# Expert 0's weights in smaller loads, and its first down product taken by halves of the contraction

## The chip, the cores and the metric

The kernel runs on one core of a Trainium2 chip. The metric is the device time of one execution in microseconds. Each comparison uses executions of both kernels, in rounds on the same chip. A ratio below is the mean time of one kernel's fast runs over the mean of the other's in the same rounds, so it is not quite the ratio of the medians that are quoted beside it.

## The reference, cut to what matters

```python
# q, k, v: 8 batches x 8 heads x 576 positions x 64
ret = (q @ k.T / 8) * decay ** (i - j)    # lower triangle only
x = (ret @ v) as 4608 tokens x 512
p = domain_probs / domain_probs.sum(-1)   # 4608 x 4
for e in range(4):                        # w1[e]: 512 x 1024, w2[e]: 1024 x 512
    h = relu(x @ w1[e])                   # "up"
    out += p[:, e] * (h @ w2[e])          # "down"
```

The kernel does batch 0's attention first (the head of the program, some 18 us), then the experts on the first tile of 512 tokens, with later batches' attention mixed in. Expert 0's weights are therefore the first that TensorE asks for, and they come from memory while the raw q, k and v of batch 0 are still arriving.

## The kernel before

```python
def load_w1(e, f=slice(0, F)):            # f32 in memory, bf16 as written
    return nc.gpsimd.dma_start(out=w1_sb[e][:, :, f], in_=moe_w1[e][:, f]...)

def load_w2(e):                           # all 8 blocks fc of 128 rows at once
    return nc.gpsimd.dma_start(out=wx[e // 2][:, (e % 2) * NFC:(e % 2 + 1) * NFC, ...], in_=moe_w2[e]...)
# ...
def down_plain(h, t, e, ns):              # ns: token group of 128; two groups share a PSUM tile
    m, g = divmod(ns, 2)
    if g == 0:
        acc0["po"] = ring_tile("po", [128, 2, Dm])
    po = acc0["po"]
    for fc in range(NFC):                 # 8 matmuls of 512 columns
        nc.tensor.matmul(po[:, g, :], lhsT=h[:, e * NFC + fc, ns * 128:(ns + 1) * 128],
                         rhs=wx[e // 2][:, (e % 2) * NFC + fc, ...], start=(fc == 0), stop=(fc == NFC - 1))
    if g == 0:
        return
    # ... both groups are scaled by p and added to the accumulator on VectorE
# ...
load_w1_at = {1: (0, slice(0, F // 2)), 2: (0, slice(F // 2, F))}   # after the casts of units 1 and 2
# ... after the head, all on GpSimd's queue:
load_w2(0)
# p0
load_w1(1)
# prb, tables
load_w2(1)
# ...
```

The up product of expert 0 begins in halves of 256 tokens, on blocks 0 to 3 of w1; blocks 4 to 7 follow, and after them the down product of four token groups.

Of the kernel before, what the change touches and what calls it, by code (L numbers as in the profile page):

```python
# [23 lines left out]
def kernel(  # L24
# [10 lines left out]
    nc = tc.nc  # L35
    B, H, S, D = q.shape
    N, E = moe_domain_probs.shape
    _, Dm, F = moe_w1.shape
# [8 lines left out]
    NFC = F // 128  # L47
# [18 lines left out]
    def ring_tile(name, shape, dt=FP32):  # L66
        return ring.tile(shape, dt, tag="ring", name=name)
# [26 lines left out]
    wx = [const.tile([128, KH, 2, HF], BF16, name=f"wx{i}") for i in range(2)]  # L94
# [4 lines left out]
    def load_w1(e, f=slice(0, F)):  # L99
        return nc.gpsimd.dma_start(out=w1_sb[e][:, :, f], in_=moe_w1[e][:, f].rearrange("(dc p) f -> p dc f", p=128))  # L100

    def load_w2(e):
        return nc.gpsimd.dma_start(
            out=wx[e // 2][:, (e % 2) * NFC:(e % 2 + 1) * NFC, :, :].rearrange("p a b c -> p a (b c)"),
            in_=moe_w2[e].rearrange("(fc p) d -> p fc d", p=128))

    early = ctx.enter_context(ExitStack())
    epool = early.enter_context(tc.tile_pool(name="epool", bufs=1))
# [24 lines left out]
    def warm(n):  # L133
        w = ring_tile("w", [128, 512])
        for _ in range(n):
            nc.tensor.matmul(w, lhsT=zz[:, 0:128], rhs=zz, start=True, stop=True)
# [249 lines left out]
    def down_plain(h, t, e, ns):  # L386
        m, g = divmod(ns, 2)
        if g == 0:
            acc0["po"] = ring_tile("po", [128, 2, Dm])
        po = acc0["po"]  # L390
        for fc in range(NFC):
            nc.tensor.matmul(po[:, g, :], lhsT=h[:, e * NFC + fc, ns * 128:(ns + 1) * 128],  # L392
                             rhs=wx[e // 2][:, (e % 2) * NFC + fc, :, :].rearrange("p a b -> p (a b)"),
                             start=(fc == 0), stop=(fc == NFC - 1))
        if g == 0:
            return
        if e == 0:
            acc0[m] = spool.tile([128, 2, Dm], FP32, tag="S", name="acc0")
        for g in range(2):
            pe = pm0[:, 2 * m + g, e:e + 1]  # L400
            if e == 0:
                nc.vector.tensor_scalar_mul(acc0[m][:, g, :], po[:, g, :], pe)
            else:
                nc.vector.scalar_tensor_tensor(acc0[m][:, g, :], po[:, g, :], pe, acc0[m][:, g, :], op0=MULT, op1=ADD)
        if e == E - 1:
            for g in range(2):
                n0 = t * NT + (2 * m + g) * 128
                nc.sync.dma_start(out=out[n0:n0 + 128, :], in_=acc0[m][:, g, :])
# [242 lines left out]
    us[0].cast("v", nc.gpsimd)  # L651
    us[0].trans_pe()
    warm(3)
    load_w1_at = {1: (0, slice(0, F // 2)), 2: (0, slice(F // 2, F))}
    def cast_unit(u):
        us[u].cast("k", nc.vector)
        us[u].cast("q", nc.vector)
        us[u].cast("v", nc.gpsimd)
        if u in load_w1_at:
            load_w1(*load_w1_at[u])  # L660

    cast_unit(1)
    us[0].scores()
    warm(4)
# [3 lines left out]
    for u in range(NU):  # L668
        if u + 2 < NU:
            cast_unit(u + 2)  # L670
        if u == NU - 1:
            part = UpHalf(0)
            part.matmuls(0)
        us[u].values_own()
        if u + 1 < NU:
            us[u + 1].scores()
        us[u].values_carried()
        if u + 2 < NU:
            us[u + 2].trans_pe(1)
        if u + 1 < NU:  # L680
            us[u + 1].kv()
# [3 lines left out]
    h = hp.tile([128, E * NFC, NT], BF16, name="h")  # L685
# [11 lines left out]
    for g in range(2):  # L697
        kv1 = opool.tile([128, 2, 2, 4, D], BF16, tag="o", name=f"kv1_{g}")
        for n in "kqv":
            a = bfs[g][n][:, :, :, :].rearrange("p c j d -> p (c j d)").rearrange("p (r h d) -> p r h d", r=2, h=4)  # L700
# [9 lines left out]
    def load_v(u):  # L710
        load_unit({n: raws[u][n].rearrange("p (h x) -> p h x", h=4) for n in "kqv"}, 1, vs[u].hf, vs[u].g, nc.gpsimd)

    load_w2(0)
    nc.gpsimd.dma_start(out=p0, in_=moe_domain_probs[0:NT, :].rearrange("(g p) e -> p g e", p=128))
    load_w1(1)
    nc.gpsimd.dma_start(out=prb, in_=moe_domain_probs.rearrange("(p t) e -> p t e", p=128))
    later_tables()
    load_w2(1)
    load_rem(0, nc.gpsimd)
    load_w1(2)  # L720
    load_w2(2)
    load_v(0)
    load_v(1)
# [53 lines left out]
    for e in range(E):  # L777
        for i in range(4):
            if e > 0 or i > 1:
                up_group(h, 0, e, i)  # L780
            run(slots, n)
            n += 1
        for m in range(4):
            down_plain(h, 0, e, m)
            run(slots, n)
            n += 1
# [13 lines left out]
    for b in range(2, B):  # L800
        g = NS * (b - 3)
# [24 lines left out]
    for t in range(1, n_nt):  # L826
        d = [Down(h, t, s) for s in range(2)]
# [46 lines left out]
```

## Time and profile before

| quantity | before |
|---|---|
| time, median of the three runs at the start | 535.12 us |
| span of the profiled execution | 533.5 us |
| TensorE busy | 526.2 us, granted clock 1.0 |
| first w1 matmul / first down product start | 18.04 / 25.68 us |
| waits of TensorE on a weight | none |

The prediction shows the busy shares, the list of TensorE's waits and its timeline. What it gives in words only are three rows of the DMA view (tile, source, queue, count, KB as written, us from issue to landing), for the two halves of w1 and for w2 of expert 0, each from a narrow window around its issue:

```profile
w<-in_moe_w_dram POOLq DMA_DIRECT2D x1, 512.0 KB, 7.9
...
w<-in_moe_w_dram POOLq DMA_DIRECT2D x1, 512.0 KB, 7.7
...
wx<-in_moe_w_dram POOLq DMA_DIRECT2D x1, 1024.0 KB, 10.5
```

Added to the issues at 9.76, 12.50 and 15.03 us they give the landings: 17.66, 20.2 and 25.53. Subtract each from the start of the first matmul that reads it, and the margins are 0.38, 2.0 and 0.15 us.

### The profile page before, as it was taken

To read this page: it belongs to the slowest core of one execution; us is meant where nothing else is said; L and a number is where in the kernel's file an instruction comes from. 1 tells how busy PE (TensorE), PEld (TensorE's weight loads), DVE (VectorE), ACT (ScalarE), POOL (GpSimd) and SP (SyncE) were. 2 spreads that over 40 slices of the span, in tenths; PEclk is the share of its full clock that TensorE was granted. 3 is DMA by queue.
4 is the path that set the end of the run, shared out by engine and by line. 5 is a ranking of instruction groups with operands and counts; after the bars stand their busy time and mean duration, and the time that the engine had idled before them with its cause. 6 is when DMAs were issued, how large, how long until landed. Compare 5 with 4: busy or idle time off the path is not lost.

```text
span 533.5 us, 10230 instructions
## 1 busy us (share of the span) xinstructions
PE 526.2 (99%) x4260; PEld 342.0 (64%) x4260; DVE 361.4 (68%) x456; ACT 85.9 (16%) x175; POOL 146.8 (28%) x189
## 2 busy tenths in 40 slices
PE   8999999999999999999999999999999999999997
PEld 4644544478745985478646865587548844884486
DVE  5436768895577667697578767776765567557763
ACT  4723440012101111020101101100110000000010
POOL 5743104235235334235132514153000000000000
PEclk9999999999999999999999999999999999999999
DMA  9999947867778866736353666454010111110001
GB/s 241 198 217 245 244 122 191 166 154 163 150 166 155 176 142 148 153 83 162 108 135 94 144 139 114 104 118 126 20 41 25 56 39 41 41 41 20 1 24 56
DMA packets 144510, 63.55 MB, mean 119 GB/s; under 512 B 123728, under 2 KB 135264, under 8 KB 144464
## 3 DMA queue, kind: packets, MB, share of 16 engines
q1 hardware_dynamic: 134080, 43.42, 36.1%
q0 software_dynamic: 10240, 19.35, 16.2%
q8 instruction: 33, 0.54, 0.4%
q10 hardware_dynamic: 144, 0.13, 0.1%
q14 instruction: 13, 0.11, 0.1%
HBM read 53.56 MB, written 9.51 MB: 118 GB/s over the span
## 4 chain that ended last, share of the span: by engine, by line
PE 73%; ACT 2%; DVE 0%; issue 0%
PE ph L357 37%; PE pd L469 34%; ACT xt L290 2%; PE o L282 1%; PE o L277 1%; PE py L469 1%; DVE h L363 0%; PE or L342 0%; PE sr L336 0%; PE or L344 0%; DVE ob L497 0%
## 5 line engine op out<-in xcount | busy, mean ns | idle before, releaser
L357 PE MATMUL ph<-xt,w 128*128 128x512 bf16 x1136 | 250.9, 379 | 0.8 <-DVE h L363 0.2
L363 DVE SCALAR_TENSOR_TENSOR h<-ph,pB 128x1024 bf16<-128x1024 f32 x128 | 156.3, 1223 | 58.1 <-PE ph L357 57.2
L357 PEld LDWEIGHTS <-w 128*128 128x128 bf16 x1136 | 109.9, 98 | 127.9
L469 PEld LDWEIGHTS <-h 128*128 128x128 bf16 x1024 | 100.0, 98 | 13.4
L469 PEld LDWEIGHTS <-s 128*128 128x128 bf16 x768 | 75.0, 98 | 8.7
L469 PE MATMUL pd<-wx,h 128*128 128x256 bf16 x512 | 61.1, 273 | 0.2
L469 PE MATMUL pd<-wx,s 128*128 128x256 bf16 x512 | 61.1, 273 | 0.0
L218 POOL DMA_DIRECT2D pB<-pd x28 | 15.7, 562 | 151.7 <-DVE h L363 150.8
L504 POOL TENSOR_TENSOR ob<-v,p 128x256 f32<-128x256 f32 x15 | 11.8, 784 | 111.8 <-DVE v L501 83.8
L237 POOL TENSOR_TENSOR bf_k<-raw_k,gk 128x512 bf16<-128x512 f32 x24 | 26.1, 1088 | 36.6 <-DMA raw_k<-in_k_dram 23.2
L269 DVE TENSOR_TENSOR sT<-s,tri 128x1024 bf16<-128x1024 f32 x24 | 28.2, 1218 | 6.4 <-PE s L267 6.4
L290 ACT ACTIVATE xt<-o 128x768 bf16<-128x768 f32 (+6 forms) x24 | 13.0, 594 | 116.8 <-PE o L282 116.8
L469 PE MATMUL pd<-t4w,h 128*128 128x256 bf16 x256 | 30.6, 273 | 0.0
L442 DVE TENSOR_TENSOR s<-s,h 128x1024 bf16<-128x1024 bf16 x32 | 29.9, 973 | 0.0
L392 PE MATMUL po<-wx,h 128*128 128x512 bf16 x128 | 29.1, 379 | 0.0
L469 PE MATMUL pd<-t2w,s 128*128 128x256 bf16 x240 | 28.7, 273 | 0.0
L469 PE MATMUL pd<-t3w,h 128*128 128x256 bf16 x240 | 28.6, 273 | 0.0
L477 ACT ACTIVATE p<-pd 128x256 f32<-128x256 f32 x16 | 6.1, 383 | 138.8 <-PE pd L469 106.2
L237 POOL TENSOR_TENSOR bf_q<-raw_q,gq 128x512 bf16<-128x512 f32 x24 | 26.6, 1109 | 5.0 <-DMA rawr_v<-in_v_dram 2.1
L446 DVE TENSOR_TENSOR s<-h,s 128x1024 bf16<-128x1024 bf16 x32 | 26.4, 863 | 0.0
L440 DVE TENSOR_TENSOR s<-h 128x1024 bf16<-128x1024 bf16 x32 | 23.7, 779 | 0.0
L486 DVE TENSOR_TENSOR u<-pd,p 128x256 f32<-128x256 f32 x15 | 6.4, 424 | 22.4 <-PE pd L469 22.3
(160 smaller groups left out, 376.4 us busy)
## 6 DMA issues: line engine op xcount, KB each, us to landing
pB<-pd POOLq DMA_DIRECT2D x28, 256.0 KB, 3.6
raw_k<-in_k_dram SPq DMA_DIRECT2D x48, 128.0 KB, 2.6
raw_q<-in_q_dram SPq DMA_DIRECT2D x48, 128.0 KB, 2.9
raw_v<-in_v_dram SPq DMA_DIRECT2D x48, 128.0 KB, 3.3
wx<-in_moe_w_dram POOLq DMA_DIRECT2D x4, 1024.0 KB, 14.5
out_dram<-oa SPq DMA_DIRECT2D x16, 256.0 KB, 2.4
out_dram<-ob SPq DMA_DIRECT2D x15, 256.0 KB, 2.2
w<-in_moe_w_dram POOLq DMA_DIRECT2D x3, 1024.0 KB, 13.8
```

The source lines that it names most:

```text
L218: eng.dma_start(out=pB[t, e], in_=pd[e:e + 1, t * NT:(t + 1) * NT].to_broadcast([128, NT]))
L237: eng.tensor_tensor(bfs[p % 2][n], raw1[n], g[:, :, 2 * p:2 * p + 2].unsqueeze(3).to_broadcast([128, NC, 2, D]), op=MULT)
L269: nc.vector.tensor_tensor(sT[:, :, :, :].rearrange("p j c t -> p (j c) t"), s[:, :, :, :].rearrange("p j c t -> p (j c) t"), tri[:, :].uns ...
L290: nc.scalar.activation(xt_of(t)[:, self.ps, n0 + a - t * NT:n0 + z - t * NT], o[:, :, a:z], Copy)
L357: nc.tensor.matmul(ph[:, f, :], lhsT=w1_sb[e][:, dc, fc * 128:(fc + 1) * 128], rhs=x[:, dc, :], start=(dc == 0), stop=(dc == NDC - 1))
L363: nc.vector.scalar_tensor_tensor(h[:, fk:fk + 2, :], ph, 0.0, pB[t, e][:, :].unsqueeze(1).to_broadcast([128, 2, NT]), op0=MAX, op1=MULT)
L392: nc.tensor.matmul(po[:, g, :], lhsT=h[:, e * NFC + fc, ns * 128:(ns + 1) * 128], rhs=wx[e // 2][:, (e % 2) * NFC + fc, :, :].rearrange("p ...
L440: nc.vector.tensor_tensor(self.alloc("s1")[:, l], h[:, l, self.b], h[:, r, self.b], op=ADD)
L442: nc.vector.tensor_tensor(self.alloc("s2")[:, l], self.s1[:, l], h[:, l, self.a], op=SUB)
L446: nc.vector.tensor_tensor(self.alloc("s4")[:, l], h[:, r, self.a], self.s2[:, l], op=SUB)
L469: mm = nc.tensor.matmul(dst, lhsT=src[:, kk, tok], rhs=rhs(c), start=(start and c == 0), stop=(c == KH - 1), skip_group_check=True)
L504: nc.gpsimd.tensor_tensor(self.ob[:, HF:Dm], self.v, self.p5, op=ADD)
```

## The change

The intent: no matmul should need more of expert 0's weights than it reads. The first piece of w1 is halved, w2 comes in two pieces, and the first down product asks for the lower half of w2 first.

```diff
-    def load_w2(e):
+    def load_w2(e, lo=0, hi=NFC):
...
-        for fc in range(NFC):
-            nc.tensor.matmul(po[:, g, :], lhsT=h[:, e * NFC + fc, ns * 128:(ns + 1) * 128],
+        if e == 0 and m == 0:
+            todo = [(gg, fc) for gg in range(2) for fc in range(4 * g, 4 * g + 4)]
+        else:
+            todo = [(g, fc) for fc in range(NFC)]
+        for gg, fc in todo:
+            nc.tensor.matmul(po[:, gg, :], lhsT=h[:, e * NFC + fc, (2 * m + gg) * 128:(2 * m + gg + 1) * 128],
...
-    load_w1_at = {1: (0, slice(0, F // 2)), 2: (0, slice(F // 2, F))}
+    load_w1_at = {1: (slice(0, F // 4),), 2: (slice(F // 4, F // 2), slice(F // 2, F))}
...
-    load_w2(0)
+    load_w2(0, 0, NFC // 2)
+    load_w2(0, NFC // 2, NFC)
```

More of the change, by code (lines that the diff above doesn't have):

```diff
@@ L100, in load_w1 @@
         return nc.gpsimd.dma_start(out=w1_sb[e][:, :, f], in_=moe_w1[e][:, f].rearrange("(dc p) f -> p dc f", p=128))
-    def load_w2(e):
+    def load_w2(e, lo=0, hi=NFC):
+        c = (e % 2) * NFC
         return nc.gpsimd.dma_start(
-            out=wx[e // 2][:, (e % 2) * NFC:(e % 2 + 1) * NFC, :, :].rearrange("p a b c -> p a (b c)"),
-            in_=moe_w2[e].rearrange("(fc p) d -> p fc d", p=128))
+            out=wx[e // 2][:, c + lo:c + hi, :, :].rearrange("p a b c -> p a (b c)"),
+            in_=moe_w2[e][lo * 128:hi * 128, :].rearrange("(fc p) d -> p fc d", p=128))
     early = ctx.enter_context(ExitStack())
@@ L658, in cast_unit @@
         us[u].cast("v", nc.gpsimd)
-        if u in load_w1_at:
-            load_w1(*load_w1_at[u])
+        for f in load_w1_at.get(u, ()):
+            load_w1(0, f)
     cast_unit(1)
```

## The prediction

> **What bounds the kernel now.** I began with the page's busy shares and its slices, then took the list of everything that TensorE waited for, and then the timeline of TensorE between 18 and 47 us, where expert 0's weights are first used.
>
> ```profile
> PE 526.2 (99%) x4260; PEld 342.0 (64%) x4260; DVE 361.4 (68%) x456; ACT 85.9 (16%) x175; POOL 146.8 (28%) x189
> ...
> PEclk9999999999999999999999999999999999999999
> DMA  9999947867778866736353666454010111110001
> ```
>
> TensorE is busy for 526.2 of 533.5 us at full clock, and DMA is dense only in the first eighth. The 7.3 us that remain are the start, the last eviction and store, and a few gaps. All the gaps that the trace knows of are these (columns: engine, line, what it waited for, us in total, times, longest):
>
> ```profile
> PE w L136 <- DVE zz L129: 1.3, 1, 1.3
> PE s L558 <- ACT qkT L537: 0.5, 1, 0.5
> PE o L621 <- ACT sbd L596: 0.2, 1, 0.2
> PE o L621 <- DVE sbd L593: 0.2, 1, 0.2
> PE w L136 <- DVE sT L560: 0.2, 1, 0.2
> PE ph L357 <- DVE h L363: 0.2, 1, 0.2
> ```
>
> No line names a weight (w1 or w2) or any DMA. The sum is 2.6 us, of which 1.3 is the start. So TensorE's own stream of instructions sets the time, in the stage of expert 0 too:
>
> ```profile
> 22.22 3.62 PE L357 MATMUL ph<-xt,w 128*128 128x512 bf16 x16
> 25.68 7.07 PE L392 MATMUL po<-wx,h 128*128 128x512 bf16 x32
> 32.58 7.07 PE L357 MATMUL ph<-xt,w 128*128 128x512 bf16 x32
> 39.49 5.78 PE L392 MATMUL po<-wx,h 128*128 128x512 bf16 x26
> ```
>
> From start to start, 32 matmuls take 39.49 - 32.58 = 6.91 us, 216 ns each. The first 32 down products take 32.58 - 25.68 = 6.90 us, and the 16 before them 25.68 - 22.22 = 3.46 us, also 216 ns each. There is no hole at the first down product.
>
> The change is aimed at a real near miss, though. The issues of expert 0's loads, from GpSimd's timeline, and the rows for single issues in the DMA view (size in KB as written to SBUF, us from issue to landing):
>
> ```profile
> 9.76 0.89 POOL L100 DMA_DIRECT2D w<-in_moe_w_dram  x1
> ...
> 12.50 0.77 POOL L100 DMA_DIRECT2D w<-in_moe_w_dram  x1
> ...
> 15.03 0.89 POOL L103 DMA_DIRECT2D wx<-in_moe_w_dram  x1
> ```
>
> The first half of w1 takes 7.9 us and lands at 17.66; it is first used at 18.04. The second takes 7.7 and lands at 20.2; first used at 22.22 (weight load at 22.11). w2 of expert 0 takes 10.5 and lands at 25.53, and the down product starts at 25.68. TensorE's weight-load row shows how close that is:
>
> ```profile
> 25.60 1.04 PEld L392 LDWEIGHTS <-h 128*128 128x128 bf16 x6 [0.25 <-issue]
> 26.95 3.14 PEld L392 LDWEIGHTS <-h 128*128 128x128 bf16 x16 [0.31 <-ACT h L361]
> ```
>
> The weight load idled 0.25 us until just after w2 landed, and 0.31 us until the relu of the last up group (25.88 + 1.02 = 26.90). Both were absorbed behind running matmuls: their starts stayed 216 ns apart.
>
> **What the Trainium skill says.** "Perfetto Trace Analysis", section "Tensor Engine Instruction (MATMUL, LD_WEIGHTS)", says that the reported end of a matmul is estimated. That is why I count from start to start; the rows give 379 ns for one 512-column matmul where the starts are 216 apart, so this trace agrees. "TensorE: Matmul & The Clock Gate", section "Wait — 56ns, not 53.3ns?", gives 215.7 ns for that spacing when warm; the measured 216 leaves nothing to gain per matmul. "DMA: Bandwidth & Descriptors", section "Issuing engines are not separate DMA queues", says that loads from all queues share 16 engines. The trace agrees: from 9 to 12 us the hardware queue holds the engines at 285 to 293 GB/s with the raw q, k and v, and the software queue, where w1 was issued at 9.76, moves nothing; it ramps up from 12.25 to 14 as the other drains. The same page's "Specifications" puts line rate at 512 B and more. A row of a w1 quarter is 256 bf16, exactly 512 B, so the rows stay at that limit; no row of this kernel's casting loads shows that size yet.
>
> **The change part by part.**
>
> 1. w1's first half becomes two quarters, the second one issued later together with the second half. Bytes are the same; packets of the first half go from 512 (128 partitions x 4 rows) of 1 KB to 1024 of 512 B. In the steady part (14 to 17 us) the software queue moves about 200 packets of 1 KB per us on 16 engines, 80 ns each; at 25 to 28 us, 105 of 2 KB, 152 ns each. That is nearly proportional, with a fixed part of some 8 ns. The raw loads' 512 B packets, 577 per us, cost 28 ns each against some 20 if proportional, again 8 ns. So 512 more packets x 8 ns / 16 engines = 0.26 us more DMA time (estimate). The second quarter is issued at 12.50 instead of 9.76. If the first quarter has drained by then (256 KB at 0.2 MB per us is 1.3 us, from 12.4 to about 14), the queue may run dry for up to about 0.8 us before the next pieces' data flow (estimate; a new issue's lag when the queue is empty is not shown). On TensorE's path: 0, as long as the margins hold. First quarter: lands about 1.3 us sooner, some 16.4. Second quarter: needed at 19.60, expected by about 17.7 to 18.8. Second half: 20.2 becomes 20.5 to 21.3, needed at 22.11.
>
> 2. w2 of expert 0 becomes two pieces of 512 KB, same packets. The lower half should land about 2.6 us (512 KB at 0.2 MB per us) before the upper: 23.2 to 24 against 25.8 to 26.6.
>
> 3. The first two down products (32 matmuls) are reordered: contraction blocks 0 to 3 of both token groups, then 4 to 7 of both. Same 32 matmuls, same 32 weight loads, 32 x 216 ns = 6.9 us as before; the two accumulations lie in separate halves of the tile. The upper half of w2 is needed 16 x 0.216 = 3.46 us later, at 29.14, and h's last blocks at about the same time, well after 26.90. So both near misses become margins of 1.7 to 2.5 us. Value in the profiled execution: the hole that they cost, 0.0 us. In executions where w2 lands later by a few tenths, that much.
>
> 4. Two more issues on GpSimd, 0.75 to 0.9 us each by the rows above. The one at 13.3 fits into the 1.20 us that GpSimd idles before its next cast (14.47), so it costs nothing. The one after 15.03 pushes p0's load, w1 of expert 1 and the tables 0.8 us later. The data queue is backed up then: w1 of expert 1, issued at 16.66, landed 13.8 us later at 30.46, so it is the queue and not the issue that sets its landing. It is needed at 32.5, a margin of 2.0 us, of which 0.3 to 1.1 us goes. p0, landing near 25.7, is not used for an eviction before 29.33.
>
> Sum on the path: 0.0 for the profiled state, minus 0.0 to 0.3 us of jitter that the near miss may cost in other executions (my estimate from the range of 534.94 to 535.67 over three runs). I take -0.1 us: 535.0.
>
> **The rivals.**
>
> (a) Real gain. If TensorE waited for weights in a way that the views hide, the change would give it back. For it: the landing at 25.53 beside the start at 25.68. Against: starts at 216 ns on both sides, and no weight among the waits. Even all gaps after the first memset together are 1.3 us, so 533.8 is the floor of this rival.
>
> (b) A new wait takes over. The smaller packets and a queue run dry push every later weight by more than 1.1 us, and the second half of w1 (margin 1.9) or expert 1's w1 (margin 2.0) lands late. For it: the software queue is saturated from 13 to 52 us, so delays are carried on. Against: it needs twice my estimate, and a wait would be the excess over the margin, perhaps 0.5 us: 535.6.
>
> (c) The raw loads of q, k, v arrive sooner because less of w1 competes, and the attention head of the program shortens. Against: w1 moves nothing before 12.25 us, when raw 3 is almost through, and TensorE there waits on ACT and DVE. Worth under 0.2 us.
>
> (d) The number of outstanding software loads. In the trace, GpSimd's waits look like a limit of eight in flight (the ninth issue waits for the landing of the first, again and again). Two more loads shift the pairs by two for expert 0 only, and w1 of expert 2 still waits for w1 of expert 1. No change: 535.1.
>
> **Range and chances.** Main course 534.8 to 535.3; rival (a) pulls to 533.9, rival (b) to 536; run spread before was 0.7 us. So 534.2 to 535.9 should hold it 8 times in 10. A change of 2% would be 10.7 us. Nothing in the first 60 us could give that, since the gaps sum to 1.3 us, and a loss would need a stall of TensorE ten times my worst delay. So 1% each.
>
> **What the profile of the changed kernel would show.** Down product starts at 25.68 give or take 0.1 and takes 6.9 us; the idle of 0.25 and 0.31 us in the weight-load row before it is gone (steps 2 and 3). The first w1 quarter lands near 16.4, the lower half of w2 near 23.5 (steps 1 and 2). w1 of expert 1 lands at 30.8 to 31.6 and no wait on it appears at 32.58 (step 4). TensorE's busy time stays within 0.5 us of 526.2. The prediction would be wrong if starts of matmuls between 18 and 40 us spread, above all at 19.60, 22.22 or 32.58, or if something outside this stretch moved.

## The result, and the profile after

The changed kernel takes 535.37 us (median of 6 runs, 535.10 to 536.56), the kernel before 535.47 us (6 runs, 534.94 to 536.39). The ratio is 0.9999, 95% interval 0.9986 to 1.0013: the same.

The timeline of TensorE in the changed kernel, against the rows that the prediction shows of before (start, duration, engine, line, operation; these lines are numbered one to five higher in this kernel):

```profile
18.50 1.05 PE L379 MATMUL ph<-xt,w 128*128 128x256 bf16 x8
...
22.68 3.62 PE L358 MATMUL ph<-xt,w 128*128 128x512 bf16 x15
26.13 7.07 PE L397 MATMUL po<-wx,h 128*128 128x512 bf16 x32
33.04 7.07 PE L358 MATMUL ph<-xt,w 128*128 128x512 bf16 x31
```

Everything is 0.45 us later than before, from the first w1 matmul on (18.50 against 18.04), and nothing is gained or lost after it: 33.04 - 26.13 = 6.91 us for the first 32 down products, as before. The shift is older than any weight. It is one new line in the list of TensorE's waits:

```profile
PE pt L540 <- DVE bf_k L529: 0.4, 1, 0.4
...
PE po L397 <- issue: 0.2, 1, 0.2
```

The first line is the transpose of unit 1 at 8.73 us, waiting for the cast of a raw k that came 5.5 us after its issue instead of 4.9. The first w1 load of this kernel is issued at 10.24. The second line is no wait. The group before the product counts 15 matmuls where the program has 16; from 22.68 to 26.13 are 3.45 us, 16 x 216 ns. The record of the last matmul is missing, and its time looks idle. The same shows on the page:

```profile
PE 524.2 (98%) x4221; PEld 342.2 (64%) x4260; DVE 360.4 (67%) x456; ACT 86.0 (16%) x175; POOL 147.3 (28%) x191
```

There are 4260 weight loads but 4221 matmuls: 39 records are missing, and with them some 2 us of "busy".

The weight-load row, which before had idle times of 0.25 and 0.31 us around the first down product, has none now:

```profile
25.92 6.79 PEld L397 LDWEIGHTS <-h 128*128 128x128 bf16 x32
```

The loads, from GpSimd's timeline (x2 is two issues in one row):

```profile
10.24 0.90 POOL L100 DMA_DIRECT2D w<-in_moe_w_dram  x1
...
12.91 1.51 POOL L100 DMA_DIRECT2D w<-in_moe_w_dram  x2
...
15.40 1.48 POOL L104 DMA_DIRECT2D wx<-in_moe_w_dram  x2
...
17.60 0.77 POOL L100 DMA_DIRECT2D w<-in_moe_w_dram  x1
```

Their rows in the DMA view, each from a narrow window around its issue:

```profile
w<-in_moe_w_dram POOLq DMA_DIRECT2D x1, 256.0 KB, 6.2
...
w<-in_moe_w_dram POOLq DMA_DIRECT2D x1, 256.0 KB, 5.0
...
w<-in_moe_w_dram POOLq DMA_DIRECT2D x1, 512.0 KB, 6.8
...
wx<-in_moe_w_dram POOLq DMA_DIRECT2D x1, 512.0 KB, 8.8
...
wx<-in_moe_w_dram POOLq DMA_DIRECT2D x1, 512.0 KB, 10.6
...
w<-in_moe_w_dram POOLq DMA_DIRECT2D x1, 1024.0 KB, 14.1
```

The second of two issues starts some 0.75 us after the first; issue plus landing time gives the table. "Needed" is the start of the first matmul that reads the piece. (The pieces of w1 are read by the weight load, up to 0.2 us before the matmul: 22.11 and 22.22, 32.37 and 32.58 before. Their margins are smaller by that much.)

| piece | before: landed, needed, margin | after: landed, needed, margin |
|---|---|---|
| w1, first quarter | 17.66 (half), 18.04, 0.38 | 16.44, 18.50, 2.1 |
| w1, second quarter | 17.66 (half), 19.60, 1.9 | 17.9, 20.06, 2.1 |
| w1, second half | 20.2, 22.22, 2.0 | 20.5, 22.68, 2.2 |
| w2, lower half | 25.53 (whole), 25.68, 0.15 | 24.2, 26.13, 1.9 |
| w2, upper half | 25.53 (whole), 26.54, 1.0 | 26.7, 27.86, 1.1 |
| w1 of expert 1 | 30.46, 32.58, 2.1 | 31.7, 33.04, 1.3 |

The thin margins grew to 2 us and the later ones shrank, but no margin was negative on either side. That is where the change went: into slack.

### The profile page after: what moved, and what is told of

Read it like the earlier page. It is cut to its first block, busy times and chain, and to the rows that moved or that the text cites. A ratio compares the mean times of both kernels' runs of the same rounds, so it can differ in the third digit from the quotient of the medians.

```text
span 534.0 us, 10194 instructions
## 1 busy us (share of the span) xinstructions
PE 524.2 (98%) x4221; PEld 342.2 (64%) x4260; DVE 360.4 (67%) x456; ACT 86.0 (16%) x175; POOL 147.3 (28%) x191
## 3 DMA queue, kind: packets, MB, share of 16 engines
q0 software_dynamic: 10784, 19.35, 16.4%
## 4 chain that ended last, share of the span: by engine, by line
PE 73%; ACT 2%; issue 0%; DVE 0%
PE ph L358 36%; PE pd L474 34%; ACT xt L291 2%; PE o L283 1%; PE o L278 1%; PE py L474 1%; DVE h L364 0%; PE or L343 0%; PE sr L337 0%; PE or L345 0%; DVE ob L502 0%
## 5 line engine op out<-in xcount | busy, mean ns | idle before, releaser
L238 POOL TENSOR_TENSOR bf_k<-raw_k,gk 128x512 bf16<-128x512 f32 x24 | 26.3, 1097 | 33.4 <-DMA raw_k<-in_k_dram 14.5
L447 DVE TENSOR_TENSOR s<-s,h 128x1024 bf16<-128x1024 bf16 x32 | 32.4, 1052 | 0.0
L451 DVE TENSOR_TENSOR s<-h,s 128x1024 bf16<-128x1024 bf16 x32 | 23.4, 773 | 0.0
```

The source lines that it names most:

```text
L238: eng.tensor_tensor(bfs[p % 2][n], raw1[n], g[:, :, 2 * p:2 * p + 2].unsqueeze(3).to_broadcast([128, NC, 2, D]), op=MULT)
L447: nc.vector.tensor_tensor(self.alloc("s2")[:, l], self.s1[:, l], h[:, l, self.a], op=SUB)
L451: nc.vector.tensor_tensor(self.alloc("s4")[:, l], h[:, r, self.a], self.s2[:, l], op=SUB)
```

## The experiments

The theory after the result: **margin, not time**. TensorE never waited for expert 0's weights, so a change that only moves their landings is worth nothing, unless something makes them late. Rivals: the change gives with one part and takes with the other; the near miss of w2 costs time in executions that were not profiled; the change itself delays the head.

### The changed kernel once more

No edit. Five runs beside the kernel before.

> The changed kernel as it is, once more. Theory (margin, not time): ratio 1.000 within 0.2%. Its first down product shows no wait, and the start of the first w1 matmul lies anywhere between 17.85 and 18.85 us, the spread of the nine traces so far, set by when the raw q, k and v of the first units land, before any weight moves: so the later head (18.50 against 18.04) in the first trace of the changed kernel was chance. Rival 1 (the change delays the head): again 18.4 or later. Rival 2 (the kernel before loses time in some executions by late w2, so its slowest runs are slower): the kernel before shows runs above 538 us here and this one none.

Measured: 535.09 us median (534.92 to 535.32) against 535.15 (11 runs, 534.94 to 537.32); ratio 0.9992, interval 0.9976 to 1.0008. TensorE in this trace:

```profile
17.71 1.05 PE L379 MATMUL ph<-xt,w 128*128 128x256 bf16 x8
...
25.35 7.07 PE L397 MATMUL po<-wx,h 128*128 128x512 bf16 x32
```

The same kernel now starts its first w1 matmul at 17.71, earlier than the kernel before did in its trace and just outside the range that I had named. Over the traces that start lies between 17.71 and 18.85 us. So the later head in the first trace was chance, and the rival that the change causes it falls: the mean start is 18.14 us over the eight traces with expert 0's loads in smaller pieces and 18.17 over the six with w1 in halves. The rival of slow runs is not shown: the kernel before had one run at 537.32, none above 538.

### Each part alone

Smaller loads with the product in its old order (the `todo` edit undone):

> Loads in smaller pieces, first down product in its old order. Theory: ratio 1.000 within 0.2%; the fifth matmul of the first product needs the upper half of w2 0.86 us after its start, and the upper half lands 0.6 to 1.2 us later than the whole did (26.3 with the head taken out, against 25.53), so this kernel is at the edge: a wait of 0 to 0.3 us. Rival (a gain of the smaller loads cancelled by a loss of the order, or the reverse): a ratio off 1.000 by over 0.2%, opposite in sign to that of the order alone.

Measured: 535.17 us median (535.05 to 537.03, 6 runs); ratio 1.0000, interval 0.9983 to 1.0016; no wait on a weight.

New order with w1 in halves and w2 as one load (the load edits undone):

> Loads as before, first down product by halves of the contraction. Theory: ratio 1.000 within 0.2%; w2 lands at about 25.5 as a whole and the first matmul is at the edge as before (wait 0 to 0.2 us), but the idle of the weight load for the last relu is gone. Rival as for the smaller loads alone, opposite sign.

Measured: 535.68 us median (534.96 to 537.65, 6 runs); ratio 1.0007, interval 0.9989 to 1.0025; no wait on a weight. Neither part gains or loses 0.3%, so there is no sign of a gain and a loss that cancel. The weight-load rows tell which part removed the second idle time (0.31 us); smaller loads alone, then order alone:

```profile
26.99 5.30 PEld L393 LDWEIGHTS <-h 128*128 128x128 bf16 x26 [0.31 <-ACT h L362]
```

```profile
25.68 6.79 PEld L396 LDWEIGHTS <-h 128*128 128x128 bf16 x32
```

With the old order the weight load still idles 0.31 us for the last relu of h; with the new order it does not. The first idle time (0.25 us) is gone in both. With the order alone the change has no part in that: w2, still whole, landed at 25.22 (15.22 + 10.0) in this trace and was needed at 25.89, so the near miss of 0.15 us was itself a matter of the execution. Neither idle time was worth anything that the times show.

### Making w2 late: the half dose

If margin is what the change buys, it must show when w2 is late. Half of expert 1's w1 (512 KB) is put ahead of expert 0's w2, in four kernels: the kernel before, the changed kernel, and each part alone.

```diff
+    load_w1(1, slice(0, F // 2))
     load_w2(0)                        # or its two pieces
     # p0
-    load_w1(1)
+    load_w1(1, slice(F // 2, F))
```

The kernel before, with the dose:

> The kernel before, with the first half of expert 1's w1 (512 KB as written) put ahead of expert 0's w2 in the software queue; the second half stays at the old place. Theory (the change buys margin, not time; the first down product waits for w2 as soon as w2 is late): w2 landed at 25.53 and was needed at 25.68; 512 KB at about 0.2 MB per us is 2.6 us, so w2 lands at about 28.1 and the time grows by 2.3 to 2.7 us, to about 537.9. A wait of that size shows at the first down product. Rival (w2's landing is not what the down product waits for): no change in time.

Measured: 539.16 us median (537.72 to 539.86, 4 runs) against 535.36; ratio 1.0064, interval 1.0042 to 1.0086. The wait, and TensorE's rows after it:

```profile
PE po L392 <- DMA wx<-in_moe_w_dram: 2.5, 1, 2.5
```

```profile
28.23 8.75 PE L392 MATMUL po<-wx,h 128*128 128x512 bf16 x32 [2.48 <-DMA wx<-in_moe_w_dram]
36.82 7.07 PE L357 MATMUL ph<-xt,w 128*128 128x512 bf16 x31
```

The up group before it started at 22.13, so without the wait the product would have started at 22.13 + 3.45 = 25.58. It started 2.65 us later, as expected. But the 32 matmuls then took 36.82 - 28.23 = 8.59 us instead of 6.91, and that 1.68 us was not expected. The stretches of that time (the figures that matter here are the stretch and, third from the right, the granted clock of TensorE):

```profile
28.50:29.00 0.50, 0.50 (x4) 0.25 (x3) 0.43 (x3) 0.00 (x0) 0.50 (x2) 0.91 1.20 219
29.00:32.00 3.00, 3.00 (x9) 1.06 (x7) 0.09 (x1) 0.00 (x0) 1.58 (x4) 0.50 1.22 203
32.00:32.50 0.50, 0.50 (x3) 0.14 (x1) 0.00 (x0) 0.00 (x0) 0.50 (x1) 0.68 1.21 195
32.50:33.00 0.50, 0.50 (x4) 0.25 (x3) 0.00 (x0) 0.00 (x0) 0.28 (x1) 1.00 1.24 203
```

For some 3.4 us the clock was half. Wait and clock make 4.33 us, less 0.09 for an earlier head: 4.2 us, which is the growth of the span (537.7 - 533.5).

The changed kernel, with the dose:

> The changed kernel with the same delay. Theory: the lower half of w2 landed at 24.2 and was needed at 26.13, the upper at 26.74 and needed at 29.58. 2.6 us later they land at 26.8 and 29.3: a wait of about 0.6 us at the first product, none at the upper half; the time grows by 0.3 to 1.0 us and this kernel is faster than the kernel before with the same delay by 1.5 to 2.3 us (0.3 to 0.4%). Rival (the change is worth nothing even where w2 is late): it grows by 2.3 to 2.7 us as well.

Measured: 536.93 us median (535.91 to 537.66, 4 runs); ratio 1.0024, interval 1.0004 to 1.0045.

```profile
25.70 1.89 PE L397 MATMUL po<-wx,h 128*128 128x512 bf16 x8
28.27 5.34 PE L397 MATMUL po<-wx,h 128*128 128x512 bf16 x24 [0.68 <-DMA wx<-in_moe_w_dram]
33.44 7.07 PE L358 MATMUL ph<-xt,w 128*128 128x512 bf16 x31
```

The growth, 1.6 us by the medians and 1.3 by the ratio, is above the expected 0.3 to 1.0 us, and the wait is in the wrong place. The lower half came 0.16 us late (22.09 + 3.45 = 25.54); then **eight** matmuls ran, not sixteen, and TensorE waited for the upper half: 33.44 - 25.70 = 7.74 us, 0.83 more than 6.91. The reordering covers one PSUM tile (`m == 0`), which is two token groups of eight matmuls, four each on the lower half. I had counted all four groups. The clock stayed at 1.0 through both waits. The kernel was 2.2 us faster than the one before with the same dose (expected: 1.5 to 2.3), but part of that is the other's lowered clock.

Smaller loads alone, with the dose:

> Same delay, loads in smaller pieces but the first down product in its old order. Theory (both parts are needed): fc 4 of the first token group is read after 4 matmuls, 0.86 us after the start; the upper half lands about 28.9 to 29.3, so the time grows by 2.0 to 2.6 us, hardly less than for the kernel before. Rival (the smaller loads alone give the margin): it grows by under 1 us.

Measured: 537.88 us median (536.52 to 538.19, 4 runs); ratio 1.0039, interval 1.0018 to 1.0059.

```profile
26.52 1.02 PE L393 MATMUL po<-wx,h 128*128 128x512 bf16 x4 [0.57 <-DMA wx<-in_moe_w_dram]
28.96 6.20 PE L393 MATMUL po<-wx,h 128*128 128x512 bf16 x28 [1.42 <-DMA wx<-in_moe_w_dram]
```

Order alone, with the dose:

> Same delay, new order of the first down product but w2 of expert 0 loaded as one piece and w1 in halves. Theory (both parts are needed): the first matmul waits for the whole of w2, landing about 28.1, so the time grows by 2.3 to 2.7 us as for the kernel before. Rival (the order alone gives the margin): it grows by under 1 us.

Measured: 536.98 us median (536.78 to 539.70, 4 runs); ratio 1.0042, interval 1.0009 to 1.0075.

```profile
27.44 7.07 PE L396 MATMUL po<-wx,h 128*128 128x512 bf16 x32 [1.33 <-DMA wx<-in_moe_w_dram]
```

Start to start, the waits at the product were 2.65 us (before), 0.16 + 0.83 (both parts), 0.74 + 1.57 (loads alone), 1.51 (order alone). In the last one the whole of w2 happened to land at 27.3 instead of 28.1, so single executions differ by 0.8 us in this, and its median grew by 1.6 us where I had expected 2.3 to 2.7. In kind the picture is clear: with the loads alone the fifth matmul stops for the upper half, with the order alone the first stops for the whole, and only both together leave about 1 us. The interval of the kernel with both parts (1.0004 to 1.0045) still touches those of the others, so the size of the difference rests on the traces more than on the times.

### Sixteen matmuls on the lower half

To test the corrected count: the changed kernel with the half dose, but the product by halves over all four token groups, in two PSUM tiles.

```diff
-        m, g = divmod(ns, 2)
+        m, g = divmod(ns, 2) if e > 0 else (ns % 2, ns // 2)
...                                   # acc0["po"] becomes acc0["po", m]
-        if e == 0 and m == 0:
+        if e == 0:
```

> The changed kernel with the half dose (512 KB of expert 1's w1 ahead of w2), but the product by halves taken over all four token groups: 16 matmuls on the lower half of w2, then 16 on the upper. In the run of the changed kernel with the half dose the wait was at the upper half: the lower was there at 25.67, eight matmuls (not the sixteen that the prediction counted) ran for 1.73 us, and the upper came at about 28.2. Theory (it is the number of matmuls on the lower half, 8, that sets the margin of the upper): with 16 of them the upper half is needed at about 29.1, after it lands, so the wait of 0.7 to 0.8 us is gone and the time is within 0.6 us of the kernel before. Rival (something else held the upper half's matmuls): the wait stays.

Measured: 536.01 us median (535.40 to 537.31, 4 runs) against 536.42 on this chip; ratio 0.9992, interval 0.9962 to 1.0021. The chip was noisier than the others (the kernel before ran from 535.28 to 539.61), and in the profiled execution the weights ahead of w2 were issued only at 18.09 us, 3 us late. TensorE's row, and GpSimd's, which waits for w2's upper half:

```profile
27.19 7.07 PE L397 MATMUL po<-wx,h 128*128 128x512 bf16 x32 [0.55 <-DMA wx<-in_moe_w_dram]
```

```profile
29.83 0.62 POOL L82 DMA_DIRECT2D rawr_v<-in_v_dram  x1 [1.38 <-DMA wx<-in_moe_w_dram]
```

The product waited for the lower half, and then ran its 32 matmuls in one piece (34.09 - 27.19 = 6.90 us), though the upper half came only at about 29.6 (19.57 + 10.0), 2.4 us after the first matmul started. After eight matmuls it would have been needed at 28.9. So the number of matmuls on the lower half is what sets the upper half's margin.

### The quarter dose

The same with a quarter of expert 1's w1 (256 KB) ahead of w2, in the kernel before and in the changed one.

> The kernel before with a smaller delay: a quarter of expert 1's w1 (256 KB in 512 B rows) ahead of expert 0's w2. At the 53 ns per row that the changed kernel's first quarters showed on 16 engines that is 1.7 us, at the rate of 1 KB rows 1.3 us. Theory: margin 0.1 us, so a wait of 1.2 to 1.6 us at the first down product and as much more time, 0.22 to 0.3%, if TensorE's clock stays full. Rival (a small lateness is absorbed elsewhere): under 0.5 us.

> The changed kernel with the smaller delay. Theory with the margin counted right (8 matmuls, 1.73 us, on the lower half): the upper half landed 26.3 when the head is taken out and comes 1.3 to 1.7 us later, at 27.6 to 28.0, needed at 27.4: a wait of 0.2 to 0.6 us, none at the lower half; the time grows by 0.1 to 0.6 us, about 1 us less than the kernel before with the same delay. With the prediction's count (16 matmuls, 3.46 us) there would be no wait at all.

Measured, on the noisy chip: 536.64 us (535.97 to 540.32) for before, ratio 1.0021, interval 0.9985 to 1.0056; 536.09 us (535.01 to 536.59) for the changed kernel, ratio 0.9986, interval 0.9962 to 1.0010. The medians do not separate them. The traces do; the kernel before, then the changed one:

```profile
26.52 7.07 PE L392 MATMUL po<-wx,h 128*128 128x512 bf16 x32 [0.56 <-DMA wx<-in_moe_w_dram]
```

```profile
25.49 7.07 PE L397 MATMUL po<-wx,h 128*128 128x512 bf16 x32
```

In the kernel before w2 landed at 26.35, 0.8 us later than without the dose and not 1.3 to 1.7, and TensorE waited 0.73 us (from 22.34 + 3.45 = 25.79): less than the 1.2 to 1.6 us expected, more than its rival's 0.5. The changed kernel waited for nothing; the 0.2 to 0.6 us that I expected there did not come, because the delay was smaller than I had worked out.

The slowest runs say more than the medians. Two of the six runs of the kernel before with this dose took 539.66 and 540.32 us, with a mean clock of 0.997 and 0.996; the other four, at 0.999 or 1.0, took 535.97 to 536.68. In the two doses without filling (the filling comes below), 6 of 14 runs with w2 in one piece had a mean clock of 0.997 or less, and none of 18 with w2 in two pieces. No trace was taken of the two here; in the traced one, the half dose above, such a clock meant some 3.4 us at half.

### Smaller still: w1 in eighths

The cost side of small loads: w1 of expert 0 in eight pieces of 128 columns.

```diff
-    load_w1_at = {1: (slice(0, F // 4),), 2: (slice(F // 4, F // 2), slice(F // 2, F))}
+    load_w1_at = {1: <eighths 0 and 1>, 2: <eighths 2 to 7>}
```

> The changed kernel with w1 of expert 0 in eighths (128 columns, rows of 256 B as written; two issued at the first place, six at the second, eight issues in all against three). Theory (small rows cost DMA time, hidden as long as the margins hold): at 13 ns of fixed cost for a row, as the quarters showed, 4096 rows against 1536 cost 2560 x 13 ns / 16 = 2.1 us more, and if 256 B rows are dearer than that, more. Five more issues of 0.75 us on GpSimd push w2's issue by about 2.5 us beyond its idle time. So the last pieces of w1 land 2 us later or more, at 22.5 against a need of 22.1 to 22.5, and the first down product's upper half 2 us later, at 28.3 against 27.4: waits of 0.3 to 1.5 us in all on w1 or w2. Rival (a row costs by its bytes alone): no wait.

Measured: one run, 536.16 us; its span is 534.5.

```profile
12.33 4.45 POOL L100 DMA_DIRECT2D w<-in_moe_w_dram  x6
17.27 1.53 POOL L104 DMA_DIRECT2D wx<-in_moe_w_dram  x2
```

```profile
28.21 5.34 PE L397 MATMUL po<-wx,h 128*128 128x512 bf16 x24 [0.57 <-DMA wx<-in_moe_w_dram]
```

Six issues in a row hold GpSimd for 4.45 us, w2 is issued at 17.27 instead of 15.40, and the upper half stops TensorE after eight matmuls (33.38 - 25.75 = 7.63 us, 0.72 over 6.91). There was no wait on w1, although I had allowed for one there too. So pieces can be too small, and the place where it showed is the load behind them.

### Filling the wait

Was the half clock a result of the idle time? The kernel before with the half dose, and 12 throwaway matmuls ahead of the product (results unchanged):

```diff
+        if e == 0 and ns == 0:
+            fill = ring_tile("fill", [128, 512])
+            for _ in range(12):
+                nc.tensor.matmul(fill, lhsT=ident, rhs=w1_sb[0][:, 0, 0:512], start=True, stop=True)
```

> The kernel before with the half dose (512 KB of expert 1's w1 ahead of w2), and 12 throwaway matmuls of 512 columns put ahead of the first down product: 12 x 216 ns = 2.6 us of work on data that is there, in the place of the wait of 2.5 us. In the profiled run of the same kernel without them TensorE idled 2.65 us, and the next 16 matmuls took 8.75 instead of 7.07 us for the group of 32, at a granted clock of 0.5 from about 28.8 to 32.3. Theory (the idle itself lowers the clock): with the idle filled, the first product still starts at about 28.2, but its group of 32 takes 7.07 us at a clock of 1.0; everything after it is 1.7 us earlier than in that run, the time 2.4 to 2.9 us above the kernel before. Rival (late w2 slows the matmuls for another reason, such as DMA traffic beside them): the group still takes about 8.7 us.

Measured: 538.07 us median (537.69 to 538.34, 6 runs) against 535.43; ratio 1.0045, interval 1.0030 to 1.0060.

```profile
25.94 2.75 PE L394 MATMUL fill<-w,ident 128*128 128x512 bf16 x12
28.53 7.07 PE L396 MATMUL po<-wx,h 128*128 128x512 bf16 x31
35.43 7.07 PE L357 MATMUL ph<-xt,w 128*128 128x512 bf16 x32
```

With the wait filled the product takes 6.90 us at a clock of 1.0, while DMA moves 206 to 232 GB/s, as much as in the stretches of half clock (203). So traffic alone does not slow the matmuls. That the idle time does is not shown by this trace: w2 landed at 27.4 in it (16.03 + 11.4), so without the filling TensorE would have idled for 1.5 us, and an idle time of 1.51 us left the clock at 1.0 in the trace of order alone with the dose. The evidence is in the runs. They are closer together: 0.65 us from lowest to highest, against 2.14 us without the filling. Of the four runs without it, the three slowest have a mean clock of 0.996 to 0.997, the fastest 0.999; with it all six have 0.999 or 1.0. That supports the idle time as the cause, without settling it.

## Why the prediction was right

- **The bound and the sum.** Right. No weight was among TensorE's waits, and a change in weight landings left the time alone: 535.37 us against 535.0 predicted, ratios 0.9999 and 0.9992. The rival of a hidden gain (a) got nothing: neither the whole change nor a part of it was faster by as much as its noise. The estimate of -0.1 us for jitter can't be told from zero in these runs.
- **Step 1, w1 in quarters.** Right within half a microsecond. First quarter at 16.44 (predicted some 16.4), second at 17.9 (17.7 to 18.8), second half at 20.5 (20.5 to 21.3). But the late head helps here: with its 0.46 us taken out, as in steps 2 and 4 below, they are 16.0, 17.5 and 20.0, the last two before the stated ranges. In the second trace, put on the same footing, they are 16.9, 17.9 and 20.5. So a delay of the second half by 0.3 to 1.1 us is not established; single executions differ by as much. The queue did run low: from 14.5 to 15.5 us it moved 0.11 MB, where the steady rate is 0.2 MB per us. The fixed part of "some 8 ns" a row held too. One engine took about 45 ns for a row of 512 B in the fuller stretches (358 rows from 14 to 15 us in the second trace) and 25 ns for 256 B (640 rows per us in the eighths). In my expectation for the eighths I had replaced it by 13 ns, from a stretch where the queue was partly dry; that was the worse figure.
- **Step 2, w2 in two pieces.** Right, with the 0.46 us of the late head taken out: 23.7 (23.2 to 24) and 26.3 (25.8 to 26.6).
- **Step 3, the order.** The mechanism was right, one term was not: "16 x 0.216 = 3.46 us later". The reordered product is the first two token groups, 16 matmuls and not 32, so it is 8 x 0.216 = 1.73 us, and the margin of the upper half is 1.1 us, where the prediction's own times (needed at 29.14, landed at 25.8 to 26.6) give 2.5 to 3.3. Its "1.7 to 2.5" is the lower half's, which measured 1.9. It cost nothing here, as 1.1 us is enough. The half dose showed the stop after eight matmuls, and the variant with sixteen removed it.
- **Step 4, two more issues.** Right. w1 of expert 1 landed at 31.7, or 31.2 without the late head (30.8 to 31.6), and its margin fell from 2.1 to 1.3 us. Rival (b), a new wait, was therefore 1.3 us away; the eighths bring one about, at w2. Rival (d) went as forecast: w1 of expert 2 still waits for w1 of expert 1 (3.72 us of GpSimd's time, 3.63 before).
- **Rival (c), a shorter head.** Nothing: 18.14 against 18.17 us in the mean of the traces.
- **The tests named in advance.** The start of the down product and "TensorE's busy time within 0.5 us of 526.2" failed (26.13; 524.2), and neither for a reason that touches the theory. The first was a late raw k; the second trace (25.35) missed the bar of 0.1 us on the other side. The bar was too narrow for a head that moves by over 1 us from run to run. Counted from the first w1 matmul, the product starts after 7.64 us before, 7.63 and 7.64 after. The second was 39 missing records.

**What stays open** is whether the near miss costs the kernel before anything in rare executions. In all rounds together, 4 of its 46 runs were above 537 us, and one of those (539.61 us) had a mean clock of 0.996, the mark that the traced run of the half dose bore (0.997), where a late w2 went with a half clock. None of the 11 runs of the changed kernel was above 536.56. With 4 in 46, none in 11 is likely enough by chance, and no trace was taken of such a run. The mark itself (0.997 or less) is found in 7 of the 72 runs of all kernels here that load w2 in one piece, and in none of the 36 that load it in two; but six of the seven had a dose.

## What to carry to other kernels

A near miss in the profile (a landing 0.15 us before its use) is not by itself a cost. Count from start to start on the bounding engine, and if there is no hole, smaller loads and a cleverer order buy margin, not time. To find out what such a margin is worth, make the load late on purpose by a known dose, in both kernels. Splitting a load brings most of its margin only if the consumer's order is split too (with the half dose, the loads alone cut the traced waits from 2.65 to 2.31 us, both parts to 0.99), and the margin of the second piece is the work that the first piece alone can feed, here eight matmuls and not sixteen: count it from the loop.

## What the Trainium skill lacked or had wrong

- "TensorE: Matmul & The Clock Gate", section "What's actually happening", lets the clock fall to half after at least one idle window of about 3.4 us. Here, if the idle time is the cause, 2.65 us was enough in a profiled run: 0.50 granted from 29 to 32 us, and 1.68 us lost on top of the wait. An idle time of 1.51 us in another run had no such effect. Whether it happens differed from run to run of one kernel (mean clock 0.996 to 0.999 in four runs).
- "DMA: Bandwidth & Descriptors", section "Specifications", gives 512 B as the least size for line rate, with no figure for loads that cast. For f32 to bf16 the time of one row on one engine was about 25 ns for 256 B as written, 45 for 512 B, 79 for 1 KB and 152 for 2 KB, which is near 8 ns plus a part in proportion to the bytes, without a step at 512 B. The f32 rows that are read are twice as long, 512 B at least, so reads below 512 B were not tried.
- No page says that matmul records can be missing from a profile while those of the weight loads are complete, and what that looks like: 39 of 4260 in every trace but the first (40 of 4272 with the filling), a false gap of 0.2 us put down to "issue", and 2 us less of busy time with the same span.
